# Eight small casts on ScalarE, moved six to nine half-slots later in a fused attention and MLP kernel

## The chip, the cores and the metric

One core of one Trainium2 chip. The metric is the device time of one execution in microseconds (us), lower is better.

## The reference, cut to what matters

```python
def _attn_ref(q, k, v, tau):            # B, N, C = 4, 6080, 256
    qn = q / (np.linalg.norm(q, axis=1, keepdims=True) + 1e-06)
    kn = k / (np.linalg.norm(k, axis=1, keepdims=True) + 1e-06)
    s = kn.transpose(0, 2, 1) @ qn / tau
    ...                                 # softmax over the last axis
    return v @ a
def _moe_ref(x, w_in, w_out, s, b):     # 24320 tokens, 256 -> 2048 -> 256
    r = np.maximum(x @ w_in, 0.0)
    g = s * (r * r) + b
    return g @ w_out
```

The last line is, with the constant taken out, `s * (r*r) @ w_out + b * sum(w_out)`; the second term, one row for all tokens, is called rowconst.

## The kernel before: the parts that matter

The tokens are done in 48 groups (g) of 512; a group has 16 hidden tiles (m), one per half-slot: half-slot 16 g + m. In each, TensorE (PE) runs two matmuls of the first layer for the current group and some of the second layer for the group before, in a seven-product scheme for 2x2 blocks. ScalarE (ACT) takes pairs of hidden tiles out of PSUM with a relu, and VectorE (DVE) or ACT squares them. Two of the seven products need T2 and T3, combinations of blocks of w_out. They are made once, near the start: DVE computes them in fp32 in the w_out pieces, and ACT casts them to fp16.

```python
ps_h = pool("ps_h", 2, space=PSUM)      # hidden tiles: two buffers of one pair each
rpool = pool("rpool", 2)                # relu results: two buffers of two pairs each
qk_pool = pool("qk_pool", 6)            # q/k chunks, and the four fp32 pieces of w_out
# ... cut ...
def combine_w(i):                       # DVE: 4 instructions of 256 columns per piece
    ...
    po(nc.vector.tensor_sub(T1[:, part, :], B12, B11))
    po(nc.vector.tensor_sub(B12, B22, B12))
    po(nc.vector.tensor_add(B11, B11, B12))
    po(nc.vector.tensor_sub(N4[:, part, :], B21, B11))

def cast_w(i):                          # ACT: 2 instructions of 256 columns per piece
    w = w_pieces[i].rearrange("p (i h) c -> p h i c", h=2)
    po(nc.scalar.copy(out=T2[:, ts(i, 2), :], in_=w[:, 0, :, :P]))
    po(nc.scalar.copy(out=T3[:, ts(i, 2), :], in_=w[:, 0, :, P:]))
# ... cut ...
for i in range(NPIECE + 1):
    at_step(11 + i, lambda i=i: rowconst_sum(i))      # DVE: fp32 sums of the w_out pieces
at_step(23, rowconst_mm)
for i in range(NPIECE):
    at_step(16 + 2 * i, lambda i=i: combine_w(i))
    at_step(21 + 2 * i, lambda i=i: cast_w(i))
# ... cut: in the loop over half-slots s, with g, m = divmod(s, 16) ...
SQUARES = {3: (0, 1, nc.scalar), 5: (1, 2, nc.scalar), 8: (2, 4, nc.vector),
           12: (4, 6, nc.vector)}
if g < NG and m % 2 == 1:
    relu(g, m // 2)                     # ACT, pair m // 2
```

`at_step(s, f)` emits f at the end of half-slot s; each engine runs what was emitted for it in that order (on ACT before, the casts of half-slot 21, at 60.99 and 61.28 us, precede the relu of half-slot 23, at 61.59). A relu of pair i writes the buffer that pairs i - 4 and their neighbours have left, so the relu of pairs 6 and 7 of group 1 waits until DVE has squared pairs 2 and 3.

## Time and profile before

| | before |
|---|---|
| median of the first three executions | 732.61 us (732.19 to 734.1) |
| profiled execution | 733.57 us, span 731.8 us, mean granted TensorE clock 0.999 |
| PE busy | 705.4 us, 96% of the span |
| ACT casts | 8 of 0.40 us, 60.99 to 66.50 us |

The times of the table include what lies outside the span of instructions (1.8 us of the profiled execution). A line of a timeline has the start, the duration, engine, source line, operation and tiles, and in brackets how long the engine had been idle before it and for what.

### The profile page before, as it was taken

How to read it: one execution, taken by the hardware profiler on the slowest of the kernel's cores; microseconds unless marked ns; L12 is line 12 of the kernel's file. 1: busy time of each engine (PE TensorE's matmuls, PEld its weight loads, DVE VectorE, ACT ScalarE, POOL GpSimd, SP SyncE). 2: the span in 40 equal slices, each digit the busy share in tenths (PEclk: the TensorE clock that was granted, in tenths of full speed). 3: DMA queues.
4: the chain of work that ended last, by engine and by line, in shares of the span. 5: the costliest groups of instructions: out<-in, count | busy, mean ns of one | idle time of the engine just before them, and what ended most of it. 6: DMA issues, size and time to landing. Idle time of an engine off the chain costs nothing.

```text
span 731.8 us, 17840 instructions
## 1 busy us (share of the span) xinstructions
PE 705.4 (96%) x7618; PEld 509.6 (70%) x7618; DVE 624.6 (85%) x873; ACT 537.8 (73%) x574; POOL 83.5 (11%) x159
## 2 busy tenths in 40 slices
PE   4798999999999999999999999999999999999997
PEld 2555777776777777776677777777668777777776
DVE  4759999988888989898888989998888888888886
ACT  5468877778777777787777777777877777777772
POOL 4532220001121110001010210000000000000000
PEclk9999999999999999999999999999999999999999
DMA  9999998236487664333667685323233333321201
GB/s 236 209 246 134 213 183 120 65 88 126 91 133 167 125 98 98 88 73 67 137 117 143 118 147 126 70 64 68 77 77 80 87 75 73 96 59 58 67 30 74
DMA packets 83664, 80.61 MB, mean 110 GB/s; under 512 B 55712, under 2 KB 58592, under 8 KB 83584
## 3 DMA queue, kind: packets, MB, share of 16 engines
q0 software_dynamic: 23536, 40.51, 33.2%
q1 hardware_dynamic: 59616, 37.64, 20.6%
q8 instruction: 60, 0.98, 0.6%
q10 hardware_dynamic: 432, 1.31, 0.5%
q14 instruction: 20, 0.16, 0.1%
HBM read 81.00 MB, written 24.90 MB: 145 GB/s over the span
## 4 chain that ended last, share of the span: by engine, by line
PE 84%; DMA 6%; ACT 4%; DVE 3%; issue 1%; POOL 1%; POOLq 0%; DVEq 0%; ACTq 0%
PE h_ps L537 40%; PE o_ps L679 37%; PE s_ps L142 4%; ACT r L547 2%; DMA w<-in_moe_w_out_dram 2%; DMA qk<-in_q_dram 2%; PE wa_ps L274 1%; DMA w_in<-in_moe_w_in_dram 1%; DMA qk<-in_k_dram 1%; ACT g L558 1%; DVE g L560 1%; ACT L247 1%; POOL qk L126 1%; PE o_ps L585 0%; DVE S L605 0%
## 5 line engine op out<-in xcount | busy, mean ns | idle before, releaser
L547 ACT ACTIVATE r<-h_ps 128x1024 f16<-128x1024 f32 (+1 forms) x384 | 388.7, 1015 | 162.7 <-PE h_ps L537 158.6
L537 PE MATMUL h_ps<-vT,wa 128*128 128x512 f16 (+7 forms) x1632 | 452.5, 364 | 5.8 <-ACT r L547 4.3
L679 PEld LDWEIGHTS <-S 128*128 128x128 f16 x2944 | 198.1, 98 | 86.6 <-issue 1.5
L679 PEld LDWEIGHTS <-g 128*128 128x128 f16 x2208 | 155.0, 98 | 74.0
L560 DVE TENSOR_TENSOR g<-r 128x2048 f16<-128x2048 f16 (+2 forms) x154 | 176.9, 1149 | 22.1 <-ACT r L547 21.7
L679 PE MATMUL o_ps<-T,S 128*128 128x128 f16 x2208 | 183.5, 219 | 1.2 <-DVE S L605 0.7
L537 PEld LDWEIGHTS <-wa 128*128 128x128 f16 x1632 | 136.5, 98 | 27.0 <-issue 6.2
L679 PE MATMUL o_ps<-w_out,g 128*128 128x128 f16 x1472 | 134.2, 219 | 0.0
L565 DVE SCALAR_TENSOR_TENSOR o_sb<-o_ps,s_out,u 128x256 f32<-128x256 f32 x138 | 66.5, 482 | 51.2 <-PE o_ps L679 49.3
L558 ACT ACTIVATE g<-r 128x1024 f16<-128x1024 f16 x92 | 96.9, 1053 | 0.0
L320 POOL DMA_DIRECT2D v<-in_v_dram x48 | 25.8, 538 | 517.2 <-DMA vT<-v 333.0
L142 PE MATMUL s_ps<-qk 128*128 128x256 f16 (+1 forms) x384 | 69.7, 281 | 14.3 <-ACT qk L133 7.1
L565 DVE SCALAR_TENSOR_TENSOR u<-o_ps,s_out,rowconst 128x256 f32<-128x256 f32 x138 | 66.0, 479 | 2.8 <-PE o_ps L679 1.6
L679 PE MATMUL o_ps<-N,g 128*128 128x128 f16 x736 | 63.5, 219 | 0.0
L679 PE MATMUL o_ps<-w_out,S 128*128 128x128 f16 x736 | 63.4, 219 | 0.0
L165 ACT ACTIVATE sq<-qk 128x1024 f16<-128x1024 f16 (+3 forms) x49 | 50.4, 1033 | 10.6 <-DMA qk<-in_k_dram 7.5
L607 DVE TENSOR_TENSOR S<-S,g 128x2048 f16<-128x2048 f16 x46 | 56.3, 1224 | 1.3
L611 DVE TENSOR_TENSOR S<-g,S 128x2048 f16<-128x2048 f16 x46 | 56.0, 1217 | 0.0
L605 DVE TENSOR_TENSOR S<-g 128x2048 f16<-128x2048 f16 x46 | 55.9, 1216 | 0.0
L609 DVE TENSOR_TENSOR S<-g 128x2048 f16<-128x2048 f16 x46 | 55.9, 1215 | 0.0
L142 PEld LDWEIGHTS <-qk 128*128 128x128 f16 (+1 forms) x384 | 32.6, 101 | 20.2 <-DVE qk L132 9.0
L162 DVE TENSOR_TENSOR sq<-qk 128x1024 f16<-128x1024 f16 (+3 forms) x49 | 33.1, 675 | 2.7 <-DMA qk<-in_q_dram 2.7
(67 smaller groups left out, 279.4 us busy)
## 6 DMA issues: line engine op xcount, KB each, us to landing
out_dram<-o_sb SPq DMA_DIRECT2D x46, 512.0 KB, 3.0
v<-in_v_dram POOLq DMA_DIRECT2D x47, 256.0 KB, 3.8
qk<-in_k_dram POOLq DMA_DIRECT2D x42, 256.0 KB, 7.0
qk<-in_q_dram POOLq DMA_DIRECT2D x42, 256.0 KB, 8.2
vT<-v SPq DMA_TRANSPOSE x182, 2.8
w<-in_moe_w_out_dram POOLq DMA_DIRECT2D x4, 512.0 KB, 14.8
raw<-in_q_dram ACTq DMA_DIRECT2D x2, 512.0 KB, 6.6
raw<-in_k_dram SPq DMA_DIRECT2D x2, 512.0 KB, 7.0
```

What stands on the lines that cost most here:

```text
L142: po(nc.tensor.matmul(self.s_ps[:, ch, :], kc[:np_, j, ts(ch, P)], qc[:np_, j, :], start=(c == 0 and j == 0 and ch == 0), stop=(c == len(s ...
L165: po(nc.scalar.activation(out=st["sq"][:np_, 1, js, :], in_=kc[:np_, js, :], func=AF.Square))
L537: po(nc.tensor.matmul(dst, wa[:, ci, ts(m, P)], src, start=(ci == 0), stop=(ci == CH - 1), skip_group_check=True))
L547: po(nc.scalar.activation(out=r16[:, :, i % 2, :n], in_=h_tiles.pop((g, i))[:, :, :n], func=AF.Relu))
L558: po(nc.scalar.activation(out=dst, in_=src, func=AF.Square))
L560: po(nc.vector.tensor_mul(dst, src, src))
L565: po(nc.vector.scalar_tensor_tensor(out=dst, in0=src, scalar=s_out, op0=ALU.mult, in1=add, op1=ALU.add))
L605: po(nc.vector.tensor_add(S[1], A21, A22))
L607: po(nc.vector.tensor_sub(S[2], S[1], A11))
L609: po(nc.vector.tensor_sub(S[3], A11, A21))
L611: po(nc.vector.tensor_sub(S[4], A12, S[2]))
L679: po(nc.tensor.matmul(st[name][:, j, :], a()[:, i, ts(j, P)], w[:, i, :], start=first, stop=last, skip_group_check=True))
```

## The change

ACT's casts stood in front of the relus on which PE waits. The change takes them out of that stretch and sets them further apart, as their results are not needed before half-slot 39.

```diff
     for i in range(NPIECE):
         at_step(16 + 2 * i, lambda i=i: combine_w(i))
-        at_step(21 + 2 * i, lambda i=i: cast_w(i))
+        at_step(27 + 3 * i, lambda i=i: cast_w(i))
```

## The prediction

Some names in it need a word: where it says that DVE squares "hidden tiles 2 and 3", pairs 2 and 3 are meant (tiles 4 to 7), "group 2's first and second relus" are those of pairs 0 and 1, and "the second to the fifth group-1 relu pair" are pairs 2 to 5. Gram matmuls and Gram squares (s_ps and sq in the lines) belong to the attention of the next batch and work on the q/k chunks. Two statements in it are looser than the trace: the DMA engines that it calls full from 68 us have a busy share of 0.84, 0.93 and 0.91 in the stretches of 2 us from there, and 1.05 or more from 74 us; and that part of a load's delay would only be time in the queue is an estimate.

> **What bounds the kernel now.** I read the page first, for the engine that is busy throughout, then the chain that ended last around the moved instructions, then the timelines of ACT, DVE and PE from 58 to 82 us. From the page:

> ```profile
> PE 705.4 (96%) x7618; PEld 509.6 (70%) x7618; DVE 624.6 (85%) x873; ACT 537.8 (73%) x574; POOL 83.5 (11%) x159
> PE   4798999999999999999999999999999999999997
> ```

> PE is busy in every slice but the first few; after about 73 us it has almost no idle time. So a microsecond that PE loses early is never got back, and one that it gains early is kept, unless something else holds the later step. All eight casts run between 60.99 and 66.50 us, in the fourth slice, the last that is under 9 tenths. The question is which engine holds PE there. DVE:

> ```profile
> 59.28 0.42 DVE L443 TENSOR_TENSOR T<-w 128x256 f16<-128x256 f32 x1
> 65.79 0.43 DVE L446 TENSOR_TENSOR N<-w 128x256 f16<-128x256 f32 x1
> 66.13 0.48 DVE L436 TENSOR_SCALAR rowconst<-rc_ps,b_bc 128x256 f32<-128x256 f32 x1
> 66.53 1.22 DVE L560 TENSOR_TENSOR g<-r 128x2048 f16<-128x2048 f16 x1
> 70.75 1.22 DVE L560 TENSOR_TENSOR g<-r 128x2048 f16<-128x2048 f16 x1 [0.56 <-ACT r L547]
> ```

> The first two lines are the ends of 16 combination instructions that DVE runs without a gap (59.28 to 66.13); the square of hidden tiles 2 and 3 of group 1 (66.53) stands behind them. ACT:

> ```profile
> 60.04 1.05 ACT L558 ACTIVATE g<-r 128x1024 f16<-128x1024 f16 x1
> 60.99 0.40 ACT L450 CAST T<-w 128x256 f16<-128x256 f32 x1
> 61.28 0.41 ACT L451 CAST T<-w 128x256 f16<-128x256 f32 x1
> 61.59 1.02 ACT L547 ACTIVATE r<-h_ps 128x1024 f16<-128x1024 f32 x1
> 66.10 0.40 ACT L451 CAST T<-w 128x256 f16<-128x256 f32 x1
> 67.84 1.02 ACT L547 ACTIVATE r<-h_ps 128x1024 f16<-128x1024 f32 x1 [1.34 <-DVE g L560]
> 68.76 1.05 ACT L165 ACTIVATE sq<-qk 128x1024 f16<-128x1024 f16 x1
> 69.70 1.93 ACT L547 ACTIVATE r<-h_ps 128x1024 f16<-128x1024 f32 x2
> 74.86 1.01 ACT L547 ACTIVATE r<-h_ps 128x1024 f16<-128x1024 f32 x1
> 77.92 1.02 ACT L547 ACTIVATE r<-h_ps 128x1024 f16<-128x1024 f32 x1 [0.18 <-PE h_ps L537]
> ```

> Two things: ACT idles 1.34 us until 67.84, because that relu needs a buffer which DVE's square has to release; and between 67.84 and 77.6 it has no other idle time than 0.41 us. It has a backlog there. PE:

> ```profile
> 62.66 0.59 PE L537 MATMUL h_ps<-vT,wa 128*128 128x512 f16 x2 [0.56 <-ACT r L547]
> 68.91 1.02 PE L537 MATMUL h_ps<-vT,wa 128*128 128x512 f16 x4 [1.91 <-ACT r L547]
> 70.77 0.59 PE L537 MATMUL h_ps<-vT,wa 128*128 128x512 f16 x2 [0.62 <-ACT r L547]
> 76.19 0.59 PE L537 MATMUL h_ps<-vT,wa 128*128 128x512 f16 x2
> ```

> These three waits, all on ACT's relus (two hidden tiles in PSUM), are PE's large ones. The first is cured by moving the casts. The second is DVE's: combinations, rowconst, square (ends 67.75), relu (67.84), PE. The chain that ended last says the same:

> ```profile
> 66.61 1.14 DVE g L560
> 67.84 1.02 ACT r L547
> 68.86 0.94 ACT sq L165
> 69.81 0.92 ACT r L547
> ```

> [...] 0.40 us each, 0.29 to 0.31 apart. A pair of casts thus costs ACT 0.60 us (60.99 to 61.59), the four pairs 2.4 us. [...] ACT's relu at 61.59 stands behind two casts that nobody needs before 76 us. [...] Here the 59 to 72 us stretch has PE gaps that DVE and ACT make.

> **The change part by part.** Nothing is removed or added; only ACT's order differs (the compiled order of DVE, PE and SP is the same but for names; POOL has two loads that wait for other buffers). Call the pairs c0 to c3. Before, they stand after the second to the fifth group-1 relu pair. After the change: c0 before the relu of 67.84; c1 behind the Gram square of 68.76, before the relu of 69.70; c2 between group 2's first and second relus (70.6 and 72.05); c3 after the ACT square of 72.97, before the Gram square of 73.92.

> Step 1, what is won. Without c0 the relu of 61.59 starts at 60.99 and PE's wait of 0.56 us at 62.66 goes. The next two relus also come earlier, and c0 falls at about 64.7. By 65 us PE is some 0.6 to 1.1 us ahead.

> Step 2, what becomes of it. DVE's run from 59.28 to 67.75 waits for nothing of ACT's that is late, so the square still ends at 67.75 and the relu still starts at 67.84. ACT's idle time before it grows from 1.34 to about 67.84 - 65.3 = 2.5 us, and PE's wait before 68.91 grows from 1.91 to about 2.5 to 3 us. Gain on the path: 0.

> Step 3, c1 on the path. After 67.84 ACT runs relu, Gram square, c1, relu. That relu moves from 69.70 to 70.30; PE's matmul of 70.77 waits for it, hence 71.37, and DVE's square of 70.75 becomes 71.35. Loss 0.60 us. DVE's following sums and evacuation, on which PE waits at about 76.0, carry the same 0.60.

> Step 4, c2 and c3 in the backlog. Group 2's second relu would start at 72.05 + 0.69 = 72.74: c1 and c2 are 1.20 late, less the 0.41 of idle time, and a start of c2 that does not abut exactly. With c3 the relu of 74.86 goes to 74.86 + 0.69 + 0.60 = 76.15. PE's matmul of 76.19 needs the PSUM tile which that relu empties; a matmul follows such a relu's start by 1.07 us (67.84 to 68.91, 69.70 to 70.77). So it starts at 76.15 + 1.07 = 77.22: 1.03 us late. Before, it had 76.19 - (74.86 + 1.07) = 0.26 us of slack, and 1.29 - 0.26 is the same 1.03.

> Step 5, afterwards. ACT's relu of 77.92, with 0.18 us idle before it, comes at about 78.95, just as its matmuls end; later ACT idles 0.78 us before a relu (79.72), so its backlog is gone. PE has no idle time for a long while, so 1.03 us stays to the end.

> Sum: 0 + 0.60 + 0.43 = about 1.0 us. 732.61 + 1.0 = 733.6 us.

> **The rivals.** A, the gain is kept: casts no longer stand before the relus and PE keeps 0.6 us or more, giving 731.5 to 732.0. For it: the wait of 0.56 us is real, and the chain does not run over the casts but over DVE, so ACT might seem free to take them later. Against it: the relu of 67.84 is held by DVE, and the new places lie where ACT has no slack.

> B, the loads get late. The w_out pieces share their six buffers with the q/k chunks, and casts release them. Chunk 3's load was issued at 68.64 and would wait for c1, about 70.4; chunk 4's, at 70.20, for c2, about 72.9. Successors of chunk 3's loads in the same semaphores are issued at 78.95 and 80.05, which I take as its landing (inferred); its first Gram matmul is at 83.64. So 3.6 us of slack against a delay of 1.8 us, and the DMA engines are full from 68 us, so that part of the delay is only time spent in the queue. Chunk 2, whose last landing is 75.88 for a use at 77.01, waits for c0, done by 65.3, and for a queue held until 67.07 anyway. If B did strike, PE would lose a further 0.5 to 2 us, giving 734 to 736.

> C, all of it is absorbed: some PE wait after 76 us, on DVE or on a transfer, was there anyway, and the time is 732.6. Against it: PE is busy 5.00 of 5 us in both stretches from 80 to 90 us. For it: executions scatter by 1.9 us (732.19 to 734.1), more than the effect.

> **Range and chances.** I give my path 60%, A 12%, B 10%, C 18%. With a scatter of some 0.7 us in the median, 8 in 10 falls in 732.3 to 734.9. Two per cent are 14.7 us; all pieces moved together are 2.4 us of ACT time, so neither side of 2% is likely: 0.5% each.

> **What would show it.** In the new timeline: the 0.56 us wait near 62.7 gone (step 1); the relu after the DVE square still near 67.84, ACT's idle time before it about 2.5 us, the PE wait at 68.9 longer (step 2); the next waiting matmul near 71.4 (step 3); a new PE wait of some 0.4 to 0.5 us on a relu near 77.2 (step 4); the same distance of 1.0 us at 100 us and at the end (step 5). I am wrong if the DVE square comes earlier than 66.5, if the matmul at 76.19 is not later, if Gram matmuls wait on a q/k load near 84 us, or if PE catches up later.

## More of the kernel before

One more line of before's DVE timeline is used further down. It is the first addition for rowconst, which waits for the pieces of w_out to land:

```profile
53.35 1.23 DVE L428 TENSOR_TENSOR acc<-w,w 128x1024 f32<-128x1024 f32 x1 [2.44 <-DMA w<-in_moe_w_out_dram]
```

## The result, and the profile after

| | before | after |
|---|---|---|
| median of six executions | 732.70 us | 734.39 us |
| lowest to highest | 732.19 to 734.38 | 733.09 to 734.83 |
| profiled span | 731.8 us | 732.8 us |
| mean granted clock in the profile | 0.999 | 0.996 |

The ratio is 1.0015, 95% interval 1.000 to 1.003: the same within 2%, and slower by about a thousandth. Ratios are the mean time of one kernel's fast runs over that of the other's of the same rounds (here 734.14 over 733.06), so they are not quite the ratio of the medians.

ACT after the change:

```profile
64.66 0.40 ACT L450 CAST T<-w 128x256 f16<-128x256 f32 x1
67.28 1.02 ACT L547 ACTIVATE r<-h_ps 128x1024 f16<-128x1024 f32 x1 [1.91 <-DVE g L560]
69.14 0.39 ACT L450 CAST T<-w 128x256 f16<-128x256 f32 x1
69.75 1.94 ACT L547 ACTIVATE r<-h_ps 128x1024 f16<-128x1024 f32 x2
72.67 1.02 ACT L547 ACTIVATE r<-h_ps 128x1024 f16<-128x1024 f32 x1 [0.39 <-PE h_ps L537]
76.10 1.01 ACT L547 ACTIVATE r<-h_ps 128x1024 f16<-128x1024 f32 x1
```

PE after the change:

```profile
68.35 1.66 PE L537 MATMUL h_ps<-vT,wa 128*128 128x512 f16 x4 [2.27 <-ACT r L547]
70.82 1.01 PE L537 MATMUL h_ps<-vT,wa 128*128 128x512 f16 x2 [0.39 <-ACT r L547]
77.16 0.59 PE L537 MATMUL h_ps<-vT,wa 128*128 128x512 f16 x2 [0.41 <-ACT r L547]
```

PE's wait of 0.56 us near 62.7 is gone. In its place ACT idles 1.91 us (1.34 before) until DVE's square is done, PE waits 2.27 us (1.91 before), and there is a new wait of 0.41 us at 77.16. That last matmul is the one of half-slot 40, at 76.19 before: 0.97 us later, and the span is 1.0 us longer.

One thing was not foreseen: the four matmuls from 68.35 took 1.66 us in place of 1.02, and the two from 70.82 took 1.01 in place of 0.59. The view of busy times by stretch tells why. Its columns are the stretch, its length, the busy time (and number of instructions) of PE, PE's weight loads, DVE, ACT and POOL, then the granted clock, the DMA share and GB/s. After the change:

```profile
65.20:68.60 3.40, 1.14 (x8) 0.52 (x6) 3.37 (x6) 1.49 (x3) 1.59 (x3) 1.00 0.36 39
68.60:72.00 3.40, 3.01 (x10) 1.24 (x9) 2.23 (x3) 3.40 (x7) 1.60 (x3) 0.50 1.06 148
```

For 3.4 us PE had half its clock. Before the change the granted clock was 1.00 throughout this part of the profile.

DVE after the change, the same two instructions as shown of before:

```profile
52.78 1.23 DVE L428 TENSOR_TENSOR acc<-w,w 128x1024 f32<-128x1024 f32 x1 [1.78 <-DMA w<-in_moe_w_out_dram]
65.97 1.21 DVE L560 TENSOR_TENSOR g<-r 128x2048 f16<-128x2048 f16 x1
```

From the start of the first addition to the end of the square it is 14.40 us (67.18 - 52.78), and before it was 14.40 us too (67.75 - 53.35). The casts do not touch DVE's run. The whole run starts when the pieces of w_out land, and that differs from execution to execution: from 51.69 to 53.35 us in the nine profiles of the table at the end of the next part. The two profiles of the kernel before have the latest two landings, but that is not the rule for it: the mean of its runs at full clock (732.47 us, below) is 1.1 us under its profiled run, which puts its usual landing at about 52.2 us, an estimate from these times, in the midst of the others.

This gives a ruler that is free of that scatter: the distance from the end of DVE's square to the start of PE's matmul of half-slot 40. It is 8.44 us before (76.19 - 67.75) and 9.98 us after (77.16 - 67.18), 1.54 more. What follows half-slot 40 does not matter: from there to the end of the span it is 655.6 us before, after, and in all the profiles of that table.

### The profile page after: what moved, and what is told of

The parts are those of the page before. It is cut to its first block, busy times and chain, and to the rows that moved or that the text cites. A ratio compares the mean times of both kernels' runs of the same rounds, so it can differ in the third digit from the quotient of the medians.

```text
span 732.8 us, 17836 instructions
## 1 busy us (share of the span) xinstructions
PE 706.4 (96%) x7618; PEld 510.0 (70%) x7618; DVE 624.5 (85%) x873; ACT 537.8 (73%) x574; POOL 83.3 (11%) x159
## 2 busy tenths in 40 slices
PE   4798999999999999999999999999999999999997
## 4 chain that ended last, share of the span: by engine, by line
PE 84%; DMA 6%; ACT 5%; DVE 4%; issue 1%; ACTq 0%; DVEq 0%; POOLq 0%
PE h_ps L537 41%; PE o_ps L679 37%; PE s_ps L142 4%; ACT r L547 2%; DMA w<-in_moe_w_out_dram 2%; PE wa_ps L274 1%; DMA w_in<-in_moe_w_in_dram 1%; DMA qk<-in_k_dram 1%; DMA raw<-in_q_dram 1%; ACT g L558 1%; DVE f L178 1%; ACT sq L165 1%; ACT L247 1%; PE o_ps L585 0%; DVE g L560 0%
## 5 line engine op out<-in xcount | busy, mean ns | idle before, releaser
L547 ACT ACTIVATE r<-h_ps 128x1024 f16<-128x1024 f32 (+1 forms) x384 | 388.6, 1015 | 163.6 <-PE h_ps L537 158.7
L537 PE MATMUL h_ps<-vT,wa 128*128 128x512 f16 (+7 forms) x1632 | 453.5, 365 | 5.6 <-ACT r L547 4.3
L560 DVE TENSOR_TENSOR g<-r 128x2048 f16<-128x2048 f16 (+2 forms) x154 | 176.7, 1148 | 23.3 <-ACT r L547 23.1
L537 PEld LDWEIGHTS <-wa 128*128 128x128 f16 x1632 | 136.7, 98 | 27.1 <-issue 6.2
L558 ACT ACTIVATE g<-r 128x1024 f16<-128x1024 f16 x92 | 96.9, 1053 | 0.0
L142 PE MATMUL s_ps<-qk 128*128 128x256 f16 (+1 forms) x384 | 70.0, 282 | 14.4 <-ACT qk L133 8.9
L165 ACT ACTIVATE sq<-qk 128x1024 f16<-128x1024 f16 (+3 forms) x49 | 50.4, 1033 | 10.3 <-DMA qk<-in_k_dram 6.3
```

Of the source, the lines that this page charges most:

```text
L142: po(nc.tensor.matmul(self.s_ps[:, ch, :], kc[:np_, j, ts(ch, P)], qc[:np_, j, :], start=(c == 0 and j == 0 and ch == 0), stop=(c == len(s ...
L165: po(nc.scalar.activation(out=st["sq"][:np_, 1, js, :], in_=kc[:np_, js, :], func=AF.Square))
L537: po(nc.tensor.matmul(dst, wa[:, ci, ts(m, P)], src, start=(ci == 0), stop=(ci == CH - 1), skip_group_check=True))
L547: po(nc.scalar.activation(out=r16[:, :, i % 2, :n], in_=h_tiles.pop((g, i))[:, :, :n], func=AF.Relu))
L558: po(nc.scalar.activation(out=dst, in_=src, func=AF.Square))
L560: po(nc.vector.tensor_mul(dst, src, src))
```

## The experiments

All gave the right result but one, which is said there. The edits are shown against the changed kernel unless another is named. The first eight were timed in five rounds each against before in two calls, the last four in a third; the median of before in the three calls was 732.54, 732.73 and 732.58 us.

**1. All casts into ACT's idle time.** Four pairs take 2.4 us of ACT; they go in front of the relu that waits for DVE.

```diff
-        at_step(27 + 3 * i, lambda i=i: cast_w(i))
+        at_step((28, 28, 28, 28)[i], lambda i=i: cast_w(i))
```

> All four pairs of casts between the relu of hidden tiles 10, 11 and the relu that waits for DVE's square, where ACT of the changed kernel idles. My theory (DVE holds that relu; the loss comes from casts behind it): ACT's order behind the DVE square is as before the change, so at full granted clock the time is that of before, 0 +- 0.3 us; ACT's idle time there falls to about 0.2 us. Rival A (the early casts cost PE 0.6 us that is kept when they leave): 0.6 us or more faster than before. Second question: the changed kernel's profile has the granted clock at 0.5 from about 68.5 to 72 us, after a PE wait of 2.3 us. If the longer wait brings that on, this kernel shows it too in most runs and is 0.7 to 1 us slower than before in those; if it is tied to the late casts, it does not.

Measured: 733.63 us median (732.68 to 734.11), ratio 1.0011 (0.9999 to 1.0023). ACT in this kernel:

```profile
67.12 0.40 ACT L451 CAST T<-w 128x256 f16<-128x256 f32 x1
67.43 1.01 ACT L547 ACTIVATE r<-h_ps 128x1024 f16<-128x1024 f32 x1
```

Here the pieces had landed early and the square ended at 66.28 us. The relu can follow a square by 0.09 us (67.84 after 67.75 in before), so the casts held it 1.06 us too long: my expectation that they fit was wrong by that. The distance is 10.48 us, 2.04 more than before. The remaining 0.98 us would be the clock, as this kernel too fell to 0.50, after a PE wait of 2.08 us. Rival A (a gain kept once the casts leave their first place) finds no support: the five times lie above the median of before. Of the second question one half came out: the half clock comes without late casts, but only two of the five runs have a mean clock of 0.997, not most, and these two are 1.4 us slower than before, not 0.7 to 1. Run 5 tests the split.

**2. The second pair back in front of the waiting relu.**

```diff
-        at_step(27 + 3 * i, lambda i=i: cast_w(i))
+        at_step((27, 28, 33, 36)[i], lambda i=i: cast_w(i))
```

> The changed kernel with the second pair back in front of the relu that waits for DVE. My theory, by terms: step 3 (0.60 us at PE's matmul near 71) is gone, steps for the third and fourth pair stay: PE's matmul on the relu of group 2's tiles 4, 5 is 0.4 us late against before, so +0.4 us at full clock, 0.6 less than the changed kernel. Rival (only the second pair matters): 0 against before. Rival B (late loads): chunk 3's load is issued 1.5 us earlier than in the changed kernel, chunk 4's as in it.

Measured: 733.11 us median (732.35 to 734.66). Profile at full clock. PE:

```profile
68.15 1.02 PE L537 MATMUL h_ps<-vT,wa 128*128 128x512 f16 x4 [1.68 <-ACT r L547]
70.01 0.59 PE L537 MATMUL h_ps<-vT,wa 128*128 128x512 f16 x2 [0.61 <-ACT r L547]
75.86 0.59 PE L537 MATMUL h_ps<-vT,wa 128*128 128x512 f16 x2 [0.27 <-ACT r L547]
```

From the first to the second line it is 1.86 us, exactly as before (68.91 to 70.77): the 0.60 us of step 3 is gone. The new wait before half-slot 40 stays, and the distance is 75.86 - 66.98 = 8.88 us, 0.44 more than before. The expectation was 0.4. On rival B I was wrong in the size: chunk 3's load is issued at 67.07, 3.1 us earlier than in the changed kernel (70.14) and not 1.5, and no matmul of either profile waits on a load.

**3. The third and fourth pair back in front of it.**

```diff
-        at_step(27 + 3 * i, lambda i=i: cast_w(i))
+        at_step((27, 30, 28, 28)[i], lambda i=i: cast_w(i))
```

> The changed kernel with the third and fourth pair back in front of the relu that waits for DVE; only the second pair stands behind it. My theory: PE's matmul near 71 is 0.60 us late against DVE's square, and that stays: +0.6 us against before at full clock, 0.4 less than the changed kernel. Rival (only the third and fourth matter): 0 against before.

Measured: 733.19 us median (732.86 to 733.95). PE, at full clock in the profile:

```profile
67.62 1.02 PE L537 MATMUL h_ps<-vT,wa 128*128 128x512 f16 x4 [1.47 <-ACT r L547]
70.09 0.59 PE L537 MATMUL h_ps<-vT,wa 128*128 128x512 f16 x2 [1.23 <-ACT r L547]
```

From line to line it is 2.47 us, 0.61 more than before: the second pair stands between the two relus. There is no wait at half-slot 40 any more. The distance is 9.46 us; 0.42 of the 1.02 more is the relu that the casts held (it started at 66.56, the square ended at 66.05 and 0.09 follows), 0.60 is the second pair. Both terms of the predicted sum are thus seen apart: 0.60 and 0.44.

**4. The changed kernel with PE kept busy in its wait.** Eight matmuls whose result nobody reads.

```diff
+    def fill_hole(n):
+        idle = ps_o.tile([P, CH, C], FP32, tag="o_ps", name="fill_ps").rearrange("p a c -> p (a c)")
+        for _ in range(n):
+            po(nc.tensor.matmul(idle, w_in16[:, 0, :P], w_in16[:, 0, :NW], start=True, stop=True,
+                                skip_group_check=True))
...
+    at_step(31, lambda: fill_hole(8))
```

> The changed kernel with eight matmuls of 512 columns, whose result nobody reads, in PE's wait for the relu behind DVE's square (they wait for rowconst, so they start at about 66 us and last 1.7 us). If the fall of the granted clock comes of PE's long wait and costs time: granted clock 0.999 or more in every run, and the slow executions (734.2 to 734.8) go: about 733.2 to 733.4 in all, 1.0 us over the quick executions of before, which is the predicted loss. If the clock costs nothing: 734.4 as the changed kernel.

Measured: 733.09 us median (732.34 to 733.57), clock 0.999 or 1.000 in all five runs. PE (source lines are shifted by the insertion):

```profile
65.77 1.89 PE L457 MATMUL fill_ps<-w_in 128*128 128x512 f16 x8
70.20 0.59 PE L544 MATMUL h_ps<-vT,wa 128*128 128x512 f16 x2 [1.23 <-ACT r L554]
76.05 0.59 PE L544 MATMUL h_ps<-vT,wa 128*128 128x512 f16 x2 [0.27 <-ACT r L554]
```

The eight took 1.89 us and not 1.7; 1.7 is an estimate that the traces allow (eight times 0.215 us, half of what four matmuls of this form, 1.02, take more than two, 0.59). The square ended at 66.56, so the distance is 9.49 us: 1.05 more than before, where the prediction's sum was 1.03. The same kernel without the filler had 9.98. The half clock is worth the other 0.49 us of that profile.

**5. All casts in the idle time, with the filler**, to split the 2.04 us of run 1. The edit is that of run 1 plus that of run 4.

> All four pairs of casts in front of the relu that waits for DVE, as in the earlier run, plus the eight unread matmuls in PE's wait. The earlier profile had PE's matmul on group 2's tiles 8, 9 start 10.48 us after the end of DVE's square (8.44 us before the change); I put 1.06 of these 2.04 us down to casts that were still running when the square ended, the rest, 0.98, to the granted clock of 0.5. If so: clock 0.999 or more, and that distance is 8.44 us plus whatever the last cast overhangs the square, within 0.1. If the clock costs nothing: still about 1 us more.

Measured: 733.23 us median (732.82 to 733.72), ratio 1.0003 (0.9989 to 1.0017). The relu started at 67.11 for a square that ended at 66.64, an overhang of 0.38 us after the 0.09. The distance is 8.81 us, and 8.44 + 0.38 = 8.82. So the 0.98 us of run 1 was the clock. Two of the five runs have a mean clock of 0.998, not the 0.999 that I expected; in the profile, one of those two, the clock is 1.00 up to 728.78 us and 0.50 from there to the end, where PE has no more work. So a mean clock of 0.998 need not mean a loss.

**6. DVE's combinations spread as well.** If DVE holds the relu, moving two pieces behind its squares must let it go.

```diff
-        at_step(16 + 2 * i, lambda i=i: combine_w(i))
-        at_step(27 + 3 * i, lambda i=i: cast_w(i))
+        at_step((16, 19, 25, 29)[i], lambda i=i: combine_w(i))
+        at_step((27, 30, 33, 36)[i], lambda i=i: cast_w(i))
```

> The changed kernel with DVE's combinations spread too: the third after the square of tiles 2, 3, the fourth after the square of tiles 4, 5. If DVE's combinations hold the relu behind which the gain of the change is lost: that relu comes about 2.5 us earlier against rowconst's predecessors, PE's wait before it falls from 2.3 to about 0.5 us or less, the clock stays full, and PE's sums (S) are the next bound; about 0.8 us faster than before, 1.8 us faster than the changed kernel at full clock. Rival (PE or ACT hold that stretch in any case, DVE's order does not matter): as the changed kernel, 733.1 to 734.8.

Measured: 732.40 us median (732.28 to 733.03), ratio 0.9994 (0.998 to 1.0008), the clock 0.999 or more in all five. DVE's square ended at 63.67, some three us earlier than in the runs above, the relu ran at 65.34 with no wait for DVE, and PE's wait before the next matmul fell from 2.27 to 0.25 us:

```profile
65.34 1.02 ACT L547 ACTIVATE r<-h_ps 128x1024 f16<-128x1024 f32 x1
```

```profile
66.42 1.02 PE L537 MATMUL h_ps<-vT,wa 128*128 128x512 f16 x4 [0.25 <-ACT r L547]
```

So DVE's order held that relu. From the first addition to that relu it is 12.63 us (14.50 in the changed kernel), so it came 1.9 us earlier, not the 2.5 that I expected. The gain over before that I expected (0.8 us) is not clear of the scatter; over the changed kernel it is 2 us by medians, part of it the clock.

**7. As run 6, the first two pairs in ACT's short waits for PE** (edit against run 6).

```diff
         at_step((16, 19, 25, 29)[i], lambda i=i: combine_w(i))
-        at_step((27, 30, 33, 36)[i], lambda i=i: cast_w(i))
+        at_step((23, 25, 33, 36)[i], lambda i=i: cast_w(i))
```

> As the run before, but the first two pairs of casts stand after the relus of tiles 6, 7 and 8, 9, where ACT waits for PE. By my count ACT's backlog behind the square is then 1.2 us shorter than in the run before; as the sums of DVE are the bound there, the time is 0 to 0.5 us lower than in it. Rival: casts before the relus cost PE (rival A), 0.6 us slower than it.

Measured: 731.93 us median (731.21 to 732.35), ratio 0.9985 (0.9971 to 0.9999). PE now waits for sums of DVE (0.69 us at 72.26), as expected. ACT still waits for PE behind both pairs (0.34 and 0.27 us), so casts in front of relus cost nothing there.

**8. The additions for rowconst on GpSimd.** As run 7, with the five additions moved from DVE to GpSimd and to half-slot 18, and the matmul on them from half-slot 23 to 25.

```diff
-            po(nc.vector.tensor_add(acc, w_pieces[0] if i == 0 else acc, w_pieces[i + 1]))
+            po(nc.gpsimd.tensor_add(acc, w_pieces[0] if i == 0 else acc, w_pieces[i + 1]))
```

> As the run before, with the five additions for rowconst (4.7 us on DVE before) on GpSimd, which waits there anyway, and rowconst's matmul two half-slots later. If DVE is the bound of the 55 to 75 us stretch: a further 0.5 to 2 us faster than the run before. If GpSimd's additions take over 3 us each or slow DVE down, PE waits for rowconst's matmul and it is slower by what they take too long.

Measured: 737.31 us median (736.65 to 738.43), ratio 1.0063, and a wrong result (relative error 0.64). The wrong result is my error: at half-slot 18 the first piece has already been overwritten by its combination. The time still tells something. GpSimd, and DVE at the same time:

```profile
55.60 2.59 POOL L428 TENSOR_TENSOR acc<-w,w 128x1024 f32<-128x1024 f32 x1 [3.37 <-DVE w L445]
```

```profile
55.89 2.58 DVE L443 TENSOR_TENSOR T<-w 128x256 f16<-128x256 f32 x1
58.57 2.40 DVE L444 TENSOR_TENSOR w<-w 128x256 f32<-128x256 f32 x1
```

Three of DVE's combinations, 0.42 us each elsewhere, last 2.40 to 2.58 us while GpSimd adds, 5.7 to 6.1 times as long. Those after GpSimd's last addition (it ends at 65.44 us) last 0.41 to 0.43 us again. What holds DVE up is not shown beyond that. PE then waited 3.89 us for rowconst's sum, and fell to half clock from 66.09 to 69.50 us. The second branch of the expectation came true.

**9. The kernel before with the filler** (five matmuls, at half-slot 31).

> The kernel before with five unread matmuls in PE's wait for the relu behind DVE's square. If executions of before fall to half clock too (its runs of 734.1 to 734.4 would be those), this kernel's runs stay below 733.6 and its clock at 0.999 or more in all; the median is that of before or up to 0.4 us lower. If that wait has nothing to do with before's spread: the same spread, 731.3 to 734.3. PE's matmul on group 2's tiles 8, 9 stays 8.44 us behind the end of DVE's square.

Measured: 732.64 us median (732.52 to 733.20), ratio 1.000 (0.9988 to 1.0013), clock 1.000 in all five. The distance is 8.44 us, as predicted. Five runs without a slow one say little by themselves, as only 6 of 33 runs of before are slow.

**10. The changed kernel with the fourth pair done twice.**

```diff
         at_step(27 + 3 * i, lambda i=i: cast_w(i))
+    at_step(36, lambda: cast_w(3))
```

> The changed kernel with the fourth pair of casts done twice, at the same place. If a pair there costs its 0.60 us one for one: PE's matmul on group 2's tiles 8, 9 is 8.44 + 1.03 + 0.60 = 10.07 us behind the end of DVE's square at full clock, about 0.5 us more if the clock falls, and the run about 0.6 us slower than the changed kernel. If ACT has slack there: as the changed kernel, 9.5 to 10.0.

Measured: 734.70 us median (733.02 to 735.75), ratio 1.0023 (1.0008 to 1.0038). The profile fell to half clock, from about 69.7 to 73.1 us. The distance is 77.08 - 66.02 = 11.06 us. My sum at full clock was 10.07; the 0.99 left over is as large as the clock's part in run 1 (0.98), but twice the 0.5 that I had allowed. Since the profile was not at full clock, this run agrees with the sum without proving it. Nor do the times: of its two runs at a clock of 1.000 one took 733.02 us and the other 734.91.

**11. Towards a better version: rowconst's sum from the fp16 copy of w_out.** It is there before the fp32 pieces, so DVE adds it in its idle time at 51 to 53 us, and the combinations start earlier (edit against the kernel before, cut at the dots).

```diff
-        if i < NPIECE - 1:
-            po(nc.vector.tensor_add(acc, w_pieces[0] if i == 0 else acc, w_pieces[i + 1]))
+        if i == 0:
+            half = spool.tile([P, NP, C], FP16, tag="S4", name="half")
+            halves.append(half)
+            po(nc.vector.tensor_add(half, w_out16[:, :NP, :], w_out16[:, NP:, :]))
+        elif i == 1:
+            po(nc.vector.tensor_add(acc, halves[0][:, :4, :], halves[0][:, 4:, :]))
...
-        at_step(16 + 2 * i, lambda i=i: combine_w(i))
-        at_step(21 + 2 * i, lambda i=i: cast_w(i))
+        at_step((14, 14, 16, 18)[i], lambda i=i: combine_w(i))
+        at_step((23, 25, 33, 36)[i], lambda i=i: cast_w(i))
```

> Towards a better version: rowconst's sum from the fp16 copy of w_out, which is there earlier, in DVE's idle time at 51 to 53 us, so that the combinations start 4 to 5 us earlier; casts after the relus of tiles 6, 7 and 8, 9, and as in the changed kernel. If DVE's backlog is what PE waits for from 62 to 72 us: PE's waits for DVE go, only one of about 0.6 us on ACT stays, and the time is 0.5 to 1 us under the version with spread combinations (731.9), so 730.9 to 731.4. If ACT is the bound then: as that version.

Measured: 731.21 us median (731.03 to 731.52), ratio 0.9979 (0.9967 to 0.9991), result correct. All of PE's waits of 0.1 us or more between 60 and 80 us:

```profile
68.00 0.59 PE L543 MATMUL h_ps<-vT,wa 128*128 128x512 f16 x2 [0.45 <-ACT r L553]
73.85 0.59 PE L543 MATMUL h_ps<-vT,wa 128*128 128x512 f16 x2 [0.27 <-ACT r L553]
```

No wait for DVE is left, and the runs scatter by 0.5 us where those of before scatter by 2.7. This is the fastest version, and faster than both kernels, if by less than 2%; fp16 addends for rowconst are part of its price.

**12. As run 11, the third and fourth pair earlier** (half-slots 27 and 33).

> As the run before, with the third pair of casts in front of the relu of tiles 12, 13 and the fourth in front of group 2's second relu. If ACT's backlog after 66 us is the bound: 0 to 0.4 us faster than the run before; if the third pair delays that relu: 0.3 to 0.6 us slower.

Measured: 731.51 us median (731.22 to 731.57), ratio 0.9982 (0.997 to 0.9994): 0.3 us slower than run 11 by medians, 0.2 by means, which is hardly more than the scatter. It leans to the second branch of the expectation; as two pairs were moved at once, which of them costs is not shown.

The profiled runs side by side, in us. "Distance" is from the end of DVE's square to PE's matmul of half-slot 40. Runs 6, 7, 11 and 12 have another order on DVE and are not on this ruler; run 8 was wrong.

| kernel | first addition | end of square | half-slot 40 | distance | half clock from 68 to 74 us |
|---|---|---|---|---|---|
| before | 53.35 | 67.75 | 76.19 | 8.44 | no |
| changed | 52.78 | 67.18 | 77.16 | 9.98 | yes |
| run 1 | 51.94 | 66.28 | 76.76 | 10.48 | yes |
| run 2 | 52.59 | 66.98 | 75.86 | 8.88 | no |
| run 3 | 51.71 | 66.05 | 75.51 | 9.46 | no |
| run 4 | 52.11 | 66.56 | 76.05 | 9.49 | no |
| run 5 | 52.23 | 66.64 | 75.45 | 8.81 | no |
| run 9 | 52.91 | 67.30 | 75.74 | 8.44 | no |
| run 10 | 51.69 | 66.02 | 77.08 | 11.06 | yes |

The first two columns differ by 14.33 to 14.45 us in all nine, wherever the casts stand.

## Why the prediction was right

The time, 734.39 us, lies in the range of 732.3 to 734.9 and above the 733.6 predicted. By the number alone that is luck: the same range holds rival C's 732.6, and 734.39 would fit rival B's 734 to 736 better than 733.6. It is the positions in the traces that tell them apart. Point by point:

- **Step 1, the early gain.** Right. The wait near 62.7 us is gone.
- **Step 2, its loss at DVE's square.** Right, and shown two ways: DVE's 14.4 us from the landing of w_out to the square are the same in nine profiles, and in run 6 the relu comes loose when DVE's order changes. ACT's idle time is 1.91 us and not 2.5, and PE's wait 2.27 and not 2.5 to 3, since in this execution w_out landed 0.57 us earlier than in the profile of before. (One reading on the way was loose: the page's last slice, with 7, is under 9 tenths too; nothing rests on it.)
- **Step 3, the second pair, 0.60 us.** Right: 0.61 us in run 3, where it stands there alone, and none in run 2, where it doesn't.
- **Step 4, the third and fourth pair, 0.43 us more.** Right: 0.44 us in run 2, and 1.05 for the whole sum of 1.03 in run 4. The way there is right too: in run 4, counted from the end of the square, group 2's second relu starts 0.69 us later than before (forecast 0.69) and the relu of pair 2 1.30 us later (forecast 1.29). The new wait before half-slot 40 was forecast at 77.22 and is at 77.16, with 0.41 us. That the absolute times agree so well is luck in part: an earlier square (0.57) and the clock (0.49) nearly cancel.
- **Step 5, nothing is caught up.** Right: 655.6 us from there to the end in every profile of the table.
- **Rival A**, a kept gain: not seen in any profile. **Rival B**, late loads: the two loads came as late as estimated, but no matmul waited on them. POOL after the change, chunks 3 and 4:

```profile
70.14 0.53 POOL L126 DMA_DIRECT2D qk<-in_k_dram  x1 [2.05 <-ACT T L451]
72.58 0.54 POOL L126 DMA_DIRECT2D qk<-in_k_dram  x1 [0.84 <-ACT T L451]
```

- **Rival C**, absorbed: wrong, by step 5.

Run 10, which fell, beside run 3, which did not though its waits were nearly the same (1.47 and 1.23 us; 1.48 and 1.23):

```profile
66.28:69.69 3.41, 1.28 (x7) 0.61 (x7) 2.24 (x4) 3.41 (x6) 1.37 (x4) 1.00 0.98 140
```

```profile
65.59:69.00 3.41, 1.80 (x10) 0.84 (x9) 2.91 (x4) 3.41 (x8) 3.28 (x7) 1.00 0.96 129
```

In run 10 one interval took in 0.91 us of the first wait and all of the second; in run 3 the edge at 69.00 left most of the second wait to the next interval. The least that PE is busy in any 3.41 us from 58 to 81 us, wherever the edges lie, is 1.24 us before and 1.15 after the change, but 2.19 in run 4, 2.01 in run 9, 1.93 in run 6 and 2.90 in run 11: set beside the 1.33 us or less before the four falls, the first two kernels are in reach of a fall, by the place of the intervals, and the other four are not. That is an estimate from these profiles; none of the other four shows a fall.

The runs, sorted by their own mean clock, show what this does to the times:

| | runs at 0.999 or more | mean | runs below | mean |
|---|---|---|---|---|
| before | 27 of 33 | 732.47 us | 6 of 33 | 734.07 us |
| changed | 2 of 6 | 733.20 us | 4 of 6 | 734.61 us |
| changed, with filler (run 4) | 5 of 5 | 733.10 us | 0 of 5 | |

A run below takes 1.4 to 1.6 us more, which is more than the 0.5 to 1.0 us of half clock on the ruler; what else comes with it is not shown (a late landing of w_out may be part of it: with the same order of casts up to that wait, it is 2.27 us in the changed kernel, with the first addition at 52.78, and 1.48 in run 10, with it at 51.69). Before has such runs too, in 18% of the 33. The change makes them more frequent, as far as six runs can say, and that is about half of the loss: the means of all runs differ by 1.38 us (734.14 against 732.76), of which 0.73 is there at full clock, and 0.94 - 0.29 = 0.65 comes of more slow runs (4/6 of 1.42, against 6/33 of 1.60). These 33 runs are of other calls than the changed kernel's six; against the six of before from its own call, whose clocks are not on record, the means differ by 1.08 us. So the median of 734.39 is one of a slow run, where the prediction's 733.6 was meant for full clock.

**What stays open.** At full clock the seven runs of the changed kernel with and without the filler average 733.13 us, 0.66 us over before (standard error 0.19), less than the 1.05 of the ruler. It may be chance, as the scatter of before's own runs is 2.2 us at full clock and the calls used different chips: run 9, with nothing on the ruler, is 0.38 us over the full-clock runs of before in its call. Or it is a part of step 1's gain that some executions keep; no profile here shows it. The runs alone don't show that the predicted 1.0 us is the loss; the ruler does. How busy PE must be to keep its clock is not shown more closely than this: intervals with 1.33 us or less were followed by half clock, and in the profiles of before and the changed kernel those with 1.60 us or more were not, for the waits of this kernel.

## What to carry to other kernels

Before moving work away from a wait, ask what the waiting instruction waits for next: here the relus could start 0.6 us earlier, but the one after them was DVE's to release, and the casts landed behind it, where ACT had no slack. Put small work where its engine idles for something else, and check that the hole is wide enough in early executions too. And count idle time of TensorE as more than its length: here four intervals of 3.41 us in which it was busy 0.60 to 1.33 us were each followed by 3.41 us at half clock, and no profile of the three kernels with a few unread matmuls in the wait shows such a fall (their 15 runs stay below 733.8 us).
